# Attention and two mixers on one core: an instruction order planned in six passes from latest starts, and the first operands loaded in three parts

## The chip, the cores and the metric

The kernel runs on one core of one Trainium2 chip. The metric is the device time of one execution in microseconds (us); less is better. The engines are named as the profile names them: PE is TensorE, DVE is VectorE, ACT is ScalarE, POOL is GpSimd, SP is the queue that issues DMA transfers.

## The reference

Three stages follow each other, all in float32, for 4 batches of 448 positions. Causal attention with 12 heads of 64 (24 pairs of heads in all) gives x of 4 x 448 x 768. A mixer follows: a product over positions (token mixing) and one over channels. Then a gated one, with a normalisation and a product over positions in between.

```python
scores = scale * q @ k^T, causal mask, softmax          # 4 x 12 heads, 448 x 448
x = attn @ v                                            # 4 x 448 x 768
u = x + (relu(x^T @ w_tok1) @ w_tok2)^T                 # 448 -> 256 -> 448
x = u + relu(u @ w_ch1) @ w_ch2                         # 768 -> 1536 -> 768
h = relu(x @ w_in); u, v = halves of h                  # 768 -> 2 x 512
v_n = (v - mean(v)) / sqrt(var(v) + 1e-6)
out = (u * (w_spatial @ v_n + b_spatial)) @ w_out       # 448 x 448, 512 -> 768
```

## The kernel before

The kernel function emits no instruction directly. It first describes all work as *jobs* of a class `Plan` (a job is one or a few instructions on one engine), with what each reads and writes, an estimated duration, a priority number and, for PSUM tiles, the banks it may use. `Plan.order()` then simulates the five queues with these estimates and gives one order of all jobs, in which they are emitted; every engine executes its own share in that order.

The simulation is one pass of list scheduling. For each engine it looks for the jobs that could start first, takes of those that could start within 0.03 us the one with the smallest priority, and does the one that starts earliest over all engines, or the one of smaller priority where starts lie within 0.1 us. A job on another engine becomes ready 0.1 us after its producer (0.25 after PE, more before PE); a transfer ends after its size over 340 GB/s and a `LANDING` of 2.8 us. A PSUM tile takes a bank when its first job starts. Some jobs have a second engine, and go where they can start better: the copies of transposed probabilities and of attention outputs are for ACT, or else for DVE. Two kinds of work are marked as sharing a port between DVE and POOL and never overlap in the plan; the small reductions' statistics (L464) are not marked.

The priorities are numbers set by hand: a pair of heads has its number n (for later pairs 1e5 and a slope), token mixing 3g + 4.5, relu and residual work of the channel part -1 (always first), weight conversions and splits offsets such as `LOW + i`, `AHEAD_OF_USE`, `WEIGHT_PRIO`.

The work in order of time, with the lines that the later steps touch:

- Attention (`scores`, `transposed`, `weighted`): for a pair, PE multiplies the four causal chunks of queries (L427, tile pss); DVE masks and takes row maxima (L436, into P and stats); ACT takes exponentials (L453); DVE adds and inverts the sums (L464, L465); POOL scales (L474); PE transposes P (L511, pst), ACT or DVE copies it (L515, L514, PT); PE multiplies by v (L613, L618, pso), and ACT (L622) or DVE (L621) copies the result to U. The operands of a pair come by one transfer into one of two stage buffers (L348): 128 partitions, 448 query columns then 448 key columns.
- The token weights come in three transfers (L318) and are unpacked on DVE (L288, L290, L292: tile psw and way) and split into a high and a low part (L329 on ACT, `lo_part`, L264, on POOL or DVE). Token mixing follows (psm).
- The channel part does batches 0 and 1 with three products of split operands (L273 to L275; uhl, hid, whl) and batches 2 and 3 by a scheme of seven products (psf), whose combined operands are built by `factors`, `weight_factors` and `gather` (raw, ts, hs; L837, L881, L931) and split in two by ACT (L868, L832) and DVE or POOL (L264; fa for weights, fb for data). L1010 adds products to U.
- The gated part: values psv, hidden pairs psf, normalisation (L1122 to L1136), the product over positions (psp, L1285), bias and gate on DVE (L1292, L1293), the last products with w_out.

PE begins with two dummy matmuls on a zeroed tile (L1351) which run while the first transfer is under way. `_layout` on the host arranges the inputs.

Of the kernel before, what the change touches and what calls it, by code (L numbers as in the profile page):

```python
# [59 lines left out]
MOVE = 0  # L60
WEIGHT_PRIO = -0.7

AHEAD_OF_USE = 9.0
LEAD, SLOPE = 14.0, 2.0

LANDING = 2.8

TOK_PRIO = 1.0

# [25 lines left out]
class Plan:  # L95
# [33 lines left out]
        return j  # L129

    def order(self):
        inf = float("inf")
# [5 lines left out]
        for j in self.jobs:  # L138
            j.left = len(j.before)
            j.ready = j.at  # L140
            for p in j.before:
                p.after.append(j)
            for b in j.bufs:
                b.left = len(b.jobs)
        engines = ("PE", "ACT", "DVE", "POOL", "SP")
        free = dict.fromkeys(engines, 0.0)
        bank_free = [0.0] * 8
# [18 lines left out]
        while done < len(self.jobs):  # L166
            best = None
            for e in engines:
                if not avail[e]:
                    continue  # L170
                starts = [(start(j, e), j) for j in avail[e]]
                first = min(s for s, _ in starts)
                if first == inf:
                    continue
                s, j = min(((s, j) for s, j in starts if s <= first + 0.03), key=lambda x: (x[1].prio, x[1].index))
                if best is None or (s, j.prio) < (best[0] - 0.1, best[1].prio) or s < best[0] + 0.1 and j.prio < best[1].prio:
                    best = (s, j, e)
            s, j, e = best
            avail[j.eng].remove(j)
            if j.other:  # L180
# [21 lines left out]
            for a in j.after:  # L202
# [6 lines left out]
                a.left -= 1  # L209
                if a.left == 0:  # L210
                    add(a)
        return sorted(self.jobs, key=lambda j: (j.start, j.index))


@with_exitstack
def mixer_kernel(ctx: ExitStack, tc: tile.TileContext, qkv, wtok, wch, wgv, wsp, bsp, out):
# [126 lines left out]
    def load(n):  # L343
        st = stage[n % 2]
        operands[n] = {"st": st}
        p = n - 2.0
        src = qkv[n // NP, n % NP]
        job("SP", 0.4, lambda: nc.sync.dma_start(st.t, src[:, : 2 * S]), w=[(st, 0)], prio=p, size=458752)  # L348
        v = buf(f"v{n % 2}", [8, D], F32, "v")
        operands[n]["v"] = v  # L350
        job("SP", 0.4, lambda: nc.sync.dma_start(v.t, src[:, 2 * S :].rearrange("p (c d) -> p c d", d=D)), w=[(v, 0)], prio=p + (0.1 if n else 1.1), size=262144)
# [5 lines left out]
    def nominal(n):  # L357
        return 0.0 if n < EAGER else START + (n - EAGER) * STEP
# [13 lines left out]
    def scores(n):  # L372
# [46 lines left out]
        def mms(some):  # L419
            for i in some:  # L420
                q0, q1 = CHUNKS[i]
                W = q1
                ks = [slice(2 * S - W, 2 * S) if n < BLOCKS else slice(S, S + W), slice(S, S + W)]
                for k, (a, c) in enumerate(terms):
                    for j in range(2):
                        r = slice(64 * j, 64 * j + 64)
                        nc.tensor.matmul(ps(i, j), a.t[r, q0:q1], c.t[r, ks[j]], start=(k == 0), stop=(k == last))  # L427
# [939 lines left out]
def _layout(inputs):  # L1367
# [66 lines left out]
```

## Time and profile before

| | us |
|---|---|
| median of 3 runs | 770.83 |
| lowest and highest | 768.9 and 773.86 |
| the profiled execution | 769.79 |
| its span from first to last instruction | 768.0 |
| busy: PE, PE's weight loads | 750.4, 642.0 |
| busy: DVE, ACT, POOL | 640.4, 427.5, 299.4 |

The mean clock granted to PE was 0.995 of its full 2.4 GHz. A timeline row gives the start, the duration, the engine, the line of the kernel, the operation, the tiles written and read, shapes, and in brackets the idle time before it with what ended it. The durations of matmuls overlap: a row of 0.37 us can be followed by the next 0.21 us later.

### The profile page before, as it was taken

The numbers are of one execution on the slowest core, as the hardware profiler recorded it, in microseconds if no ns is written. First come the engines' busy times: TensorE is split into PE (matmuls) and PEld (weight loads), VectorE is DVE, ScalarE is ACT, GpSimd is POOL, SyncE is SP. The second block draws the span as 40 slices with busy tenths as digits, with TensorE's granted clock in tenths as the row PEclk, the third lists the DMA queues.
The fourth block names the chain that finished last, engine by engine and source line by source line (L and its number), as shares of the span: only waits on it lengthen the run. The fifth ranks groups of instructions, "written<-read, shape, count | busy, mean of one in ns | idle before, by whom it ended". The sixth has DMA issues, their size and how long they took to land. (4 is left out here: it accounts for less than half of the span.)

```text
span 768.0 us, 12460 instructions
## 1 busy us (share of the span) xinstructions
PE 750.4 (98%) x4216; PEld 642.0 (84%) x4216; DVE 640.4 (83%) x1517; ACT 427.5 (56%) x1035; POOL 299.4 (39%) x354
## 2 busy tenths in 40 slices
PE   8998999999999999999999999999999999999998
PEld 4576778888887888888889899998988898888997
DVE  6989899898878978787469977999999998599482
ACT  6997676743358465452337667544564675545241
POOL 4788756466647565542310000000411050653210
PEclk9999999999999999999999999999999999999999
DMA  7683676889955896998722122421401100400113
GB/s 268 199 285 115 225 260 237 305 282 344 350 182 179 255 321 207 286 254 262 219 83 113 42 83 83 149 78 42 124 14 42 42 0 1 131 1 37 73 49 131
DMA packets 48320, 122.02 MB, mean 159 GB/s; under 512 B 4864, under 2 KB 19840, under 8 KB 47744
## 3 DMA queue, kind: packets, MB, share of 16 engines
q1 hardware_dynamic: 48256, 121.23, 47.7%
q8 instruction: 33, 0.54, 0.3%
q14 instruction: 31, 0.25, 0.1%
HBM read 91.46 MB, written 29.75 MB: 158 GB/s over the span
## 5 line engine op out<-in xcount | busy, mean ns | idle before, releaser
L275 PE MATMUL psf<-fb,fa 128*128 128x448 f32 x420 | 154.6, 368 | 2.4 <-DVE fa L264 2.3
L273 PE MATMUL psf<-fb,fa 128*128 128x448 f32 x420 | 154.6, 368 | 1.7 <-DVE U L1010 1.7
L274 PE MATMUL psf<-fb,fa 128*128 128x448 f32 x420 | 154.3, 367 | 0.0
L264 POOL TENSOR_TENSOR whl<-whl 128x768 fp32r<-128x768 f32 x45 | 82.8, 1847 | 77.8 <-ACT whl L749 70.5
L453 ACT ACTIVATE P<-P,stats 128x448 f32<-128x448 f32 (+3 forms) x192 | 95.6, 503 | 25.0 <-DVE stats L436 22.6
L474 POOL TENSOR_SCALAR P<-P,stats 128x448 f32<-128x448 f32 (+2 forms) x192 | 88.0, 477 | 36.3 <-DVE stats L465 26.0
L275 PEld LDWEIGHTS psf<-fb,fa 128*128 128x128 f32 x420 | 79.3, 189 | 10.1 <-DVE fa L264 3.5
L273 PEld LDWEIGHTS psf<-fb,fa 128*128 128x128 f32 x420 | 79.3, 189 | 9.6 <-issue 2.0
L274 PEld LDWEIGHTS psf<-fb,fa 128*128 128x128 f32 x420 | 79.3, 189 | 6.8
L868 ACT CAST fa<-raw 128x384 fp32r<-128x384 f32 (+1 forms) x112 | 56.2, 531 | 46.0 <-PE psf L275 24.9
L436 DVE CUSTOM_DVE_ANT_0 P<-pss,mask 128x448 f32<-128x448 f32 (+3 forms) x192 | 70.1, 413 | 8.8 <-PE pss L427 7.4
L264 POOL TENSOR_TENSOR wv<-wf,wv 128x512 fp32r<-128x512 f32 x6 | 8.8, 1486 | 159.6 <-DVE fb L264 152.1
L264 DVE TENSOR_TENSOR fa<-raw,fa 128x384 fp32r<-128x384 f32 (+1 forms) x109 | 62.7, 600 | 6.7 <-ACT fa L868 6.7
L273 PE MATMUL ps<-hid,whl 128*128 128x448 f32 x144 | 54.7, 380 | 1.2 <-DVE hid L267 1.1
L273 PE MATMUL ps<-uhl,whl 128*128 128x448 f32 x144 | 55.3, 384 | 0.0
L275 PE MATMUL ps<-hid,whl 128*128 128x448 f32 x144 | 52.7, 366 | 0.0
L274 PE MATMUL ps<-hid,whl 128*128 128x448 f32 x144 | 52.7, 366 | 0.0
L275 PE MATMUL ps<-uhl,whl 128*128 128x448 f32 x144 | 52.7, 366 | 0.0
L274 PE MATMUL ps<-uhl,whl 128*128 128x448 f32 x144 | 52.6, 365 | 0.0
L749 ACT CAST whl<-whl 128x768 fp32r<-128x768 f32 x45 | 37.4, 834 | 24.6 <-DMA whl<-plain 24.4
L264 POOL TENSOR_TENSOR ql<-stage,qh 128x896 fp32r<-128x896 f32 x18 | 38.1, 2118 | 24.5 <-issue 12.9
L789 DVE TENSOR_TENSOR U<-ps,U 128x448 f32<-128x448 f32 x48 | 29.8, 620 | 20.6 <-PE ps L275 19.9
(174 smaller groups left out, 1813.7 us busy)
## 6 DMA issues: line engine op xcount, KB each, us to landing
way<-in_wch SPq DMA_DIRECT2D x24, 768.0 KB, 5.5
whl<-plain SPq DMA_DIRECT2D x45, 384.0 KB, 4.5
stage<-in_qkv SPq DMA_DIRECT2D x24, 448.0 KB, 3.9
plain<-way SPq DMA_DIRECT2D x24, 384.0 KB, 3.1
raw<-plain SPq DMA_DIRECT2D x24, 384.0 KB, 3.6
round<-PB SPq DMA_DIRECT2D x7, 1024.0 KB, 6.5
PT<-round SPq DMA_DIRECT2D x28, 256.0 KB, 6.3
v<-in_qkv SPq DMA_DIRECT2D x24, 256.0 KB, 3.8
```

The costliest lines, as they stand in the source:

```text
L264: e.tensor_tensor(lo, x, hi.bitcast(F32), op=ALU.subtract)
L273: nc.tensor.matmul(ps, ah, bh, start=(first and i == 0), stop=False, **kw)
L274: nc.tensor.matmul(ps, ah, bl, start=False, stop=False, **kw)
L275: nc.tensor.matmul(ps, al, bh, start=False, stop=(last and i == n - 1), **kw)
L436: nc.vector.tensor_tensor_reduce(out=P(i)[:M, j, :], in0=ps(i, j), in1=mask[:M, S - 128 : S - 128 + W] if j == 0 and n < BLOCKS or M == 64 ...
L453: nc.scalar.activation(P(i)[:M, j, :], P(i)[:M, j, :], AF.Exp, bias=s.t[:M, 0, c : c + 1], scale=-1.0, accum_out=s.t[:M, 1, c : c + 1])
L474: nc.gpsimd.tensor_scalar(P(i)[:M, j, :], P(i)[:M, j, :], s.t[:M, 2, c : c + 1], 1.0, op0=ALU.mult, op1=ALU.mult)
L749: job("ACT", act(DM, False), lambda: nc.scalar.copy(w.t[:, 0, :], w.t[:, 1, :].bitcast(F32)), r=ks, w=ks, prio=p)
L789: job("DVE", dve(S), lambda d=d, ps=ps: nc.vector.tensor_tensor(u.t[:, d, :], ps.t[:, :S], u.t[:, d, :], op=ALU.add), r=[(ps, 0), *u_keys( ...
L868: job("ACT", act(n, False), lambda: nc.scalar.copy(part(o, 0), at(d)), r=[key(d)], w=[wk], prio=p + 0.1 * o)
```

## The change

`order()` now does six passes. Each runs the same list scheduling (now `run()`); after each, `due()` walks the finished plan backwards and gives every job the latest time at which it could start without moving the plan's end: before all that depend on it (with the latencies, and for transfers size and `LANDING`), before the next owner of its PSUM bank, and for PE before the next PE job. That time replaces the priority by hand for all five engines in the next pass (jobs marked 1e8 and above keep theirs). The first pass uses the hand-set priorities; of the six plans the one with the earliest modelled end is kept. `LANDING` goes from 2.8 to 2.3.

The operands of pair 0 come in three transfers, of 384, 256 and 256 of the 896 columns. The host puts the columns that chunks 0 and 1 use side by side into the first; `scores(0)` reads them at their new places, and only chunks 3 and 2 wait for all three.

```diff
+PASSES = 6
+DUE = "ACT", "DVE", "POOL", "SP", "PE"
-LANDING = 2.8
+LANDING = 2.3
...
+        own = {j: (j.eng, j.us, j.emit, j.prio) for j in self.jobs}
+        best = None
+        for k in range(PASSES):
+            for j in self.jobs:
+                j.eng, j.us, j.emit, _ = own[j]
+            if not self.run():
+                break
+            end = max(j.start + j.us for j in self.jobs)
+            if best is None or end < best[0]:
+                best = end, [(j.start, j.eng, j.us, j.emit) for j in self.jobs], {b: b.tag for j in self.jobs for b in j.bufs if b.banks}
+            self.due(end, own, k)
...
+    def due(self, end, own, k):
...
+        late, pe = {}, end
+        for j in reversed(jobs):
+            t = pe if j.eng == "PE" else end
+            for a in j.after:
+                lat = 0.0
+                if a.eng != j.eng or j.eng == "SP":
+                    lat = 0.25 if j.eng == "PE" else 0.1
+                    if a.eng == "PE":
+                        lat += 0.3 if j.start < START else 0.8
+                if j.eng == "SP":
+                    lat += j.size / 340e3 + LANDING
+                t = min(t, late.get(a, end) - lat)
+            for b in j.bufs:
+                if j in b.jobs:
+                    for a in later.get(b, ()):
+                        t = min(t, late.get(a, end) - 0.3)
+            late[j] = t - j.us
+            if j.eng == "PE":
+                pe = late[j]
+        for j in self.jobs:
+            if own[j][0] in DUE and own[j][3] < 1e8:
+                j.prio = late[j]
...
-        job("SP", 0.4, lambda: nc.sync.dma_start(st.t, src[:, : 2 * S]), w=[(st, 0)], prio=p, size=458752)
+        for x, (c0, c1) in enumerate(((0, 2 * S),) if n else ((256, 640), (0, 256), (640, 896))):
+            job("SP", 0.4, lambda c0=c0, c1=c1: nc.sync.dma_start(st.t[:, c0:c1], src[:, c0:c1]), w=[(st, x)], prio=p, size=512 * (c1 - c0))
...
+                qs = [slice(q0, q1)] * 2
+                if n == 0:
+                    ks[0] = slice(S - W, S)
+                    q = q0 + 256 if i < 2 else q0 - 192
+                    qs = [slice(S + q0, S + q1), slice(q, q + q1 - q0)]
...
-            job("PE", us, lambda some=some: mms(some), r=split_keys, w=[*pkeys, ("scored", n, some[0])], touch=holds, prio=n, at=nominal(n))
+            job("PE", us, lambda some=some: mms(some), r=split_keys if n or some[0] == 0 else [(st, 0), (st, 1), (st, 2)], w=[*pkeys, ("scored", n, some[0])], touch=holds, prio=n, at=nominal(n))
...
+    x, a, b = pairs[0], slice(0, 64), slice(64, 128)
+    x[a, : 2 * S] = np.concatenate([x[a, S : 2 * S], x[a, :S]], axis=1)
+    x[b, :S] = np.concatenate([x[b, 192:S], x[b, :192]], axis=1)
```

The changed file has 74 more lines, so a line of before stands at a higher number after: 427 at 497, 436 at 506, 264 at 327, 288 at 351, 464 at 534, 515 at 585, 621 and 622 at 691 and 692, 837 at 907, 881 at 951, 931 at 1001, 1010 at 1080, 1292 at 1362.

PE and POOL have as many instructions as before. ACT has five more and DVE five fewer: seven copies of pso to U go from DVE to ACT, two copies of PT go the other way in the net. SP has two more. The order changes nearly everywhere. Three places on DVE follow.

First place, the second pair of heads, some 10 us after the start. Before, DVE's queue reads (pss is the scores' PSUM tile, psw and way belong to the token weights):

```order
L465 RECIPROCAL stats0_65<-stats0_65 128x4
L290 SCALAR_TENSOR_TENSOR psw_206<-way1_152,psw_206 128x384
L292 SCALAR_TENSOR_TENSOR way1_152<-way1_152,psw_206 128x384
L436 ISA P32_220,stats1_66<-pss_186,mask_64 128x448
L436 ISA stats1_66 128x1
L288 TENSOR_SCALAR psw_225<-way1_152 128x384
L290 SCALAR_TENSOR_TENSOR psw_225<-way1_152,psw_225 128x384
L292 SCALAR_TENSOR_TENSOR way1_152<-way1_152,psw_225 128x384
L436 ISA P32_220,stats1_66<-pss_188,mask_64 128x448
```

After (the 14 rows ahead of this piece hold the other six reductions of that pair):

```order
L506 ISA P101_70,stats1_66<-pss_200,mask_64 128x192
L506 ISA stats1_66 128x1
L506 ISA P101_70,stats1_66<-pss_202,mask_64 128x192
L506 ISA stats1_66 128x1
L351 TENSOR_SCALAR psw_238<-way1_154 128x384
L353 SCALAR_TENSOR_TENSOR psw_238<-way1_154,psw_238 128x384
L355 SCALAR_TENSOR_TENSOR way1_154<-way1_154,psw_238 128x384
L584 COPY PT_240<-pst_249 128x512
```

All eight reductions of the pair come ahead of the first conversion of token weights; before, the second of the eight stood behind two such conversions.

Second place, in the seven products of batches 2 and 3, at 420 us in the trace of before. Before (raw_4823 and raw_4896 belong to the weights of the next set, the last fa to those that PE takes next):

```order
L931 TENSOR_TENSOR hs_4761<-psf_4806,hs_4761 128x448
L881 TENSOR_TENSOR raw_4823<-raw_4823 128x384 x2
L881 TENSOR_TENSOR raw_4896<-raw_4823 128x384
L931 TENSOR_TENSOR hs_4842<-psf_4735,hs_4842 128x448
L264 TENSOR_TENSOR fa_4898<-raw_4823,fa_4898 128x384
L837 TENSOR_TENSOR hs_4761<-hs_4761 128x448
L837 TENSOR_TENSOR hs_4761<-hs_4842,hs_4761 128x448
L837 TENSOR_TENSOR ts_4859<-U2_2678,ts_4731 128x448
L264 TENSOR_TENSOR fa_4717<-raw_4594,fa_4717 128x384
```

After, the same split reads fa_4719<-raw_4596:

```order
L327 TENSOR_TENSOR fb_4840<-ts_4824,fb_4840 128x448
L327 TENSOR_TENSOR fb_4845<-ts_4824,fb_4845 128x448
L327 TENSOR_TENSOR fa_4719<-raw_4596,fa_4719 128x384
L327 TENSOR_TENSOR fa_4777<-raw_4708,fa_4777 128x384
L327 TENSOR_TENSOR fa_4860<-raw_4820,fa_4860 128x384
L951 TENSOR_TENSOR raw_4596<-raw_4596,raw_4708 128x384
```

The split that PE takes next stands ahead of the combinations of the next weights and of the gathers of hs, where it stood behind them.

Third place, the product over positions of the gated part (at 685 us). Before (psp is its PSUM tile, the fa of 128x768 are splits of w_out):

```order
L1292 TENSOR_TENSOR psp_7272<-psp_7272,bias_4062 128x448
L1293 TENSOR_TENSOR gate0_6369<-psp_7272,gate0_6369 128x448
L264 TENSOR_TENSOR fa_7222<-raw_7052,fa_7222 128x768
L264 TENSOR_TENSOR fa_7224<-raw_7092,fa_7224 128x768
L1292 TENSOR_TENSOR psp_7290<-psp_7290,bias_4062 128x448
L1293 TENSOR_TENSOR gate1_6409<-psp_7290,gate1_6409 128x448
```

After:

```order
L327 TENSOR_TENSOR fa_7228<-raw_7094,fa_7228 128x768
L1362 TENSOR_TENSOR psp_7272<-psp_7272,bias_4122 128x448
L1363 TENSOR_TENSOR gate0_6378<-psp_7272,gate0_6378 128x448
L1201 RECIPROCAL bias_4122<-bias_4122 128x1
L1203 TENSOR_SCALAR bias_4122<-bias_4122 128x1
L1204 TENSOR_SCALAR bias_4122<-bias_4122 128x1
L1205 TENSOR_SCALAR bias_4122<-bias_4122 128x1
L1206 TENSOR_SCALAR vn_7163<-v_7215,bias_4122 128x512
L1362 TENSOR_TENSOR psp_7289<-psp_7289,bias_4122 128x448
L1363 TENSOR_TENSOR gate1_6411<-psp_7289,gate1_6411 128x448
```

The splits, two of which stood side by side ahead of the second gate, now stand one at a time between gates (two of the four further ahead than this piece); a chain of the normalisation (bias, then vn) has come in ahead of the last gate.

## Rows read from the trace of the kernel before

**Rows 1.** Page, part 1: busy us, share of the span, instructions.

```profile
PE 750.4 (98%) x4216; PEld 642.0 (84%) x4216; DVE 640.4 (83%) x1517; ACT 427.5 (56%) x1035; POOL 299.4 (39%) x354
```

**Rows 2.** Stretches: us; PE, PEld, DVE, ACT, POOL busy; clock, DMA, GB/s.

```profile
4.15:20.00 15.85, 14.22 (x85) 8.09 (x84) 13.42 (x57) 12.39 (x42) 6.39 (x11) 1.00 0.79 289
20.00:64.00 44.00, 41.85 (x302) 28.95 (x304) 40.99 (x136) 38.03 (x119) 35.48 (x57) 1.00 0.70 234
64.00:74.00 10.00, 8.07 (x63) 6.24 (x61) 9.44 (x39) 8.57 (x28) 8.39 (x14) 0.83 0.15 36
180.00:260.00 80.00, 78.49 (x479) 67.65 (x478) 68.27 (x160) 41.13 (x97) 54.39 (x54) 1.00 0.74 254
421.00:431.00 10.00, 8.18 (x33) 7.12 (x32) 9.18 (x18) 5.04 (x10) 0.00 (x0) 0.83 0.18 62
500.00:600.00 100.00, 97.78 (x464) 86.38 (x463) 96.40 (x191) 53.90 (x120) 14.10 (x18) 1.00 0.17 55
600.00:700.00 100.00, 98.61 (x465) 86.70 (x464) 84.49 (x183) 55.09 (x119) 40.60 (x32) 1.00 0.11 34
```

**Rows 3.** What PE waited for: line, releaser, us, times, longest.

```profile
PE pss L427 <- DVE stats L436: 2.8, 4, 1.4
PE psf L275 <- DVE fa L264: 2.3, 2, 1.8
PE psf L273 <- DVE U L1010: 1.7, 1, 1.7
PE pst L511 <- ACT U L622: 0.7, 2, 0.4
```

**Rows 4.** Timeline, the start: start us, duration us, engine, line, operation.

```profile
0.73 0.86 SPq L348 DMA_DIRECT2D stage<-in_qkv  x2
3.53 0.63 PE L1351 MATMUL zeros<-P 128*128 128x256 f32 x1
4.15 2.97 PE L427 MATMUL pss<-stage 64*64 64x64 f32 x16
```

**Rows 5.** Timeline, 18 to 21 us, DVE, ACT, PE; brackets: wait before.

```profile
18.88 0.62 DVE L621 COPY U<-pso 128x448 f32<-128x448 f32 x1
19.45 0.66 ACT L453 ACTIVATE P<-P,stats 128x448 f32<-128x448 f32 x1
20.10 1.72 PE L427 MATMUL pss<-stage 64*128 64x448 f32 x8 [1.01 <-DVE stats L436]
```

**Rows 6.** L464 by tile (ns min/median/max), then timeline around 60 us.

```profile
L464 DVE TENSOR_SCALAR stats<-stats x25: 152/170/2926, 8.5 to 334.5; 128x8 f32<-128x8 f32 x23, 128x4 f32<-128x4 f32 x2
60.08 2.93 DVE L464 TENSOR_SCALAR stats<-stats 128x8 f32<-128x8 f32 x1
60.87 1.00 POOL L264 TENSOR_TENSOR whl<-way,whl 128x384 fp32r<-128x384 f32 x1
66.12 0.61 PE L427 MATMUL pss<-qh 64*128 64x448 f32 x2 [1.38 <-DVE stats L436]
```

**Rows 7.** Timeline, 420 to 426 us, DVE and PE.

```profile
420.26 1.60 DVE L881 TENSOR_TENSOR raw<-raw 128x384 f32<-128x384 f32 x3
422.79 1.35 DVE L837 TENSOR_TENSOR hs<-hs 128x448 f32<-128x448 f32 x2
425.19 0.47 PE L275 MATMUL psf<-fb,fa 128*128 128x448 f32 x1 [1.82 <-DVE fa L264]
```

**Rows 8.** Timeline, 521 to 523 us, DVE.

```profile
521.34 1.15 DVE L837 TENSOR_TENSOR hs<-hs 128x448 f32<-128x448 f32 x2
522.41 0.61 DVE L1010 TENSOR_TENSOR U<-psf,U 128x448 f32<-128x448 f32 x1
```

**Rows 9.** Timeline, 684 to 691 us, DVE and PE.

```profile
684.26 0.95 DVE L264 TENSOR_TENSOR fa<-raw,fa 128x768 fp32r<-128x768 f32 x1
686.32 2.78 DVE L264 TENSOR_TENSOR fa<-raw,fa 128x768 fp32r<-128x768 f32 x2
690.35 0.47 PE L1285 MATMUL psp<-wsp,nhl 128*128 128x448 f32 x1 [1.04 <-DVE gate L1293]
```

More of the change, by code (lines that the diff above doesn't have):

```diff
@@ L131, in order @@
     def order(self):
-        inf = float("inf")
         for j in self.jobs:
@@ L138, in order @@
         for j in self.jobs:
+            for p in j.before:
+                p.after.append(j)
+        own = {j: (j.eng, j.us, j.emit, j.prio) for j in self.jobs}
[9 more added lines that the diff above has]
+            self.due(end, own, k)
@@ new lines, in order @@
+        for j, x in zip(self.jobs, best[1]):
+            j.start, j.eng, j.us, j.emit = x
+        for b, tag in best[2].items():
+            b.tag = tag
+        return sorted(self.jobs, key=lambda j: (j.start, j.index))
+    def due(self, end, own, k):
+        jobs = sorted(self.jobs, key=lambda j: (j.start, j.index))
+        owners = {}
+        for j in jobs:
+            for b in j.bufs:
+                if b.banks and b not in owners.setdefault(b.tag, []):
+                    owners[b.tag].append(b)
+        later = {}
+        for l in owners.values():
+            for b, c in zip(l, l[1:]):
+                later[b] = [j for j in c.jobs if not j.before.intersection(c.jobs)]
+        late, pe = {}, end
[10 more added lines that the diff above has]
+                t = min(t, late.get(a, end) - lat)
+            for b in j.bufs:
+                if j in b.jobs:
[7 more added lines that the diff above has]
+                j.prio = late[j]
@@ L139, in order, with run @@
+    def run(self):
+        inf = float("inf")
+        for j in self.jobs:
             j.left = len(j.before)
             j.ready = j.at
-            for p in j.before:
-                p.after.append(j)
             for b in j.bufs:
                 b.left = len(b.jobs)
+                if b.banks:
+                    b.tag = None
         engines = ("PE", "ACT", "DVE", "POOL", "SP")
@@ L177, in order @@
                     best = (s, j, e)
+            if best is None:
+                return False
             s, j, e = best
@@ L211, in order @@
                     add(a)
-        return sorted(self.jobs, key=lambda j: (j.start, j.index))
+        return True
 @with_exitstack
@@ L426, in mms @@
                         r = slice(64 * j, 64 * j + 64)
-                        nc.tensor.matmul(ps(i, j), a.t[r, q0:q1], c.t[r, ks[j]], start=(k == 0), stop=(k == last))
+                        nc.tensor.matmul(ps(i, j), a.t[r, qs[j]], c.t[r, ks[j]], start=(k == 0), stop=(k == last))
         for some, us in (((3, 0), 1.3 if whole else 1.05), ((2, 1), 1.2 if whole else 0.9)) if n else (((0, 1), 0.9), ((3,), 1.0), ((2,), 0.7)):
             pkeys = {(banks[j][PLACE[i][0]], 0) for i in some for j in range(2)}
-            job("PE", us, lambda some=some: mms(some), r=split_keys, w=[*pkeys, ("scored", n, some[0])], touch=holds, prio=n, at=nominal(n))
+            job("PE", us, lambda some=some: mms(some), r=split_keys if n or some[0] == 0 else [(st, 0), (st, 1), (st, 2)], w=[*pkeys, ("scored", n, some[0])], touch=holds, prio=n, at=nominal(n))
         for i in chunks:
```

## The prediction, made before the changed kernel was run

> **What bounds the kernel now.** I read the page's busy times first, then the table by stretches, then the list of what TensorE waited for, then the timelines of the places where it waited. The first shows PE busy for 750.4 of 768.0 us [rows 1]: one engine carries the span, and a plan can only win what PE stands idle or runs slowly for. The stretches [rows 2] say where. Idle time is a stretch's length less its PE busy time: 1.6 us from the first score matmul at 4.15 to 20; 2.15 in 20 to 64; 1.9 in 64 to 74; 1.5 in 180 to 260; 1.8 in 421 to 431; 2.2 in 500 to 600; 1.4 in 600 to 700. In two of them the granted clock was 0.83: 10 us at 0.83 is 3.4 us at the half level (1.2 GHz), which loses 1.7 us of work each time. The rest of PE's idle time lies before 4.15 and behind its last matmul, where the plan has nothing to move. What can be won is 12.6 us of idle time and 3.4 us of slow clock, 16.0 in all.
>
> Nearly all these waits end with a VectorE instruction [rows 3]: the row maximum of the scores (L436), the split of an operand (L264), the update of U (L1010), the gate (L1293). Yet DVE is busy 83% [rows 1], so it is seldom short of time over a long stretch; something less urgent stands ahead of what PE wants. That is what an order can mend, and the argument of my forecast.
>
> **The change part by part.** The kernel does the same arithmetic on PE and POOL with the same counts. Five more copies stand on ACT and five fewer on DVE, among them seven of U that DVE made before; what counts is the order. I sum against the profiled execution, 769.8 us (span 768.0 and 1.8 around it).
>
> *Three transfers for the first pair.* PE's last warm-up matmul ends at 3.53 + 0.63 = 4.16, and the first score matmul starts at 4.15 [rows 4]. An earlier landing finds PE still warming up: 0. The bounds: -0.6, if that warm-up's end, which is modelled, really came its whole 0.63 earlier and PE stood waiting for the load; and +0.9, because two further issues (two take 0.86 [rows 4]) push the second pair's load and the transfers of values and token weights back by 0.86 on SP's queue. I take 0, since the second pair is wanted only after the first one's matmuls, at 4.15 + 2.97 = 7.1, and the first load, issued at 0.73, was there by 4.15: some 3.4 us, which from an issue at 2.0 ends at 5.4.
>
> *Up to 64 us (1.6 + 2.15 = 3.8 us idle).* The largest wait is the 1.01 at 20.10: PE waits for a reduction of DVE, which until 19.5 was busy with a copy of U (0.62) [rows 5]. The order of before mixes token-weight conversions and such copies among pair 1's reductions; after, all of that pair's reductions come first (first place of the section on the change). But in 20 to 64 ACT is busy 38.0 of 44 us and DVE 41.0 [rows 2], so a wait removed on one can come back on the other: I take 60%, -2.3, between 0 and -3.8.
>
> *64 to 74 (1.9 idle, 1.7 of clock).* The wait of 1.38 before 66.12 followed a 2.93 us standstill of a tiny DVE instruction, L464 on 128x8, while POOL ran its two-input L264 (60.87) [rows 6]; the median of L464 is 170 ns. The planner doesn't know this stall. Only a larger lead of the reductions would hide it. The new order, which puts the reductions of a pair ahead of conversions (first place), gives such a lead, but nothing in it keeps POOL's instruction away from DVE's. I take 60%: -2.2, between 0 and -3.6.
>
> *180 to 260 (1.5).* Short waits for DVE in the channel units, none of which I looked into alone; the same 60%: -0.9, between 0 and -1.5.
>
> *421 to 431 (1.8 and 1.7 of clock).* PE waits 1.82 for one split (L264). Ahead of it DVE did three combinations of the *next* weights (1.60) and two gathers of hidden parts (1.35) [rows 7]. In the new order the awaited split stands ahead of both (second place). Moving 2.95 us behind it covers the 1.82, and without the wait the half level would not appear, which in the two stretches at 0.83 stood behind these two waits, 1.38 and 1.82 (the 1.7 in 500 to 600 brought none; the clock there reads 1.00 [rows 2]). I take all of it: -3.5. The other end is 0, if what now stands ahead becomes late itself.
>
> *500 to 600 (2.2).* The update of U at 522.41, for which PE waited 1.7 [rows 3], came behind gathers worth 1.15 [rows 8]: the same pattern, 70%: -1.5, between 0 and -2.2.
>
> *600 to 700 (1.4).* The gate that PE waited 1.04 for stands behind two 768-wide splits, 2.78 together [rows 9]. In the new order two of the four splits are already done and the others come one at a time (third place); but a normalisation chain has moved in between, and the last gate of that piece stands behind it. 65%: -0.9, between 0 and -1.4.
>
> *What is added.* Copies on ACT, later drains, stalls at other places: nothing in the trace prices these, so from 0 to 6 us; nearest to one further wait like the 1.38, I take +1.5.
>
> Sum: 0 - 2.3 - 2.2 - 0.9 - 3.5 - 1.5 - 0.9 + 1.5 = -9.8, or 760.0 us for an execution like the profiled one. The median of the runs shown, 770.83, lies 1.0 above it: 761.0.
>
> A rule speaks against the third and the seventh term. The rows: L464, 170 ns at the median, took 2.93 us beside POOL's work [rows 6]; a 768-wide split took 0.95 alone and 1.39 on average for two beside POOL [rows 9]. The Trainium skill, Advanced Engine Details and Errata, VectorE Performance Modes, Mode Summary, says that VectorE's second port to SBUF is shared with GpSimd, so that two-port Vector instructions and GpSimd ones hold each other up. By that rule the trace agrees, the standstill stays wherever the two meet, and those two terms would be 0: the sum would be -6.7.
>
> **The rivals.**
> 1. *The waits only change their names.* The first 74 us and the spatial stage are short of DVE and ACT time, and there nothing is won; 421 to 431 and 500 to 600 give 3.5 + 1.5, less a new wait of 1.5: -5.0, 765.8. For it: DVE 41.0 and ACT 38.0 of 44 us [rows 2]. Against it: the waits are few and each has a plainly postponable instruction ahead.
> 2. *Slower: U's copies queue on ACT.* ACT executes in order; seven copies that DVE made now stand behind exponentials, and a transpose waits for such a copy, as PE did twice for L622 (0.7 in sum) [rows 3]. A copy took 0.62 on DVE and an exponential of 448 columns takes 0.66 [rows 5]; behind two of these a copy ends 1.94 later. Seven such delays are 13.6, two falls of the clock 3.4; only the late gains of 5.0 remain: +12.0, 782.8. It decides from (5.0 - 3.4) / 7 = 0.23 us per copy for slower at all, and from 1.3 us for over 1%. Against it: of the 13 copies that ACT makes in the kernel before only two made PE wait, 0.4 at the longest [rows 3].
> 3. *DVE's stalls beside POOL stay, or recur.* If they stay, the two terms that hang on them are lost: 761.0 + 2.2 + 0.9 = 764.1. Each further one that lands on the path costs 1.38 and 1.7 of clock, 3.1; two more give 770.3. For it: the 2.93 above, which no plan foresaw. Against it: one such stall in the whole span of before brought the clock down.
> 4. *More than the idle time.* All 16.0 us go (754.8), and PE's busy time itself shrinks where the matmuls stand apart. For it: weight loading is busy 66% in 20 to 64 (28.9 of 44) against 87% in 600 to 700 [rows 2]; at 87% the same loads would take 44 x 0.21 = 9 us less, of which I count 2: 752.8. The Trainium skill, Perfetto Trace Analysis, Identifying the Most-Contended Engine, calls matmul busy time a poor measure and weight-load time a better one; by it the early stage has room that the idle sum doesn't show. Against it: the matmuls there have other shapes (64 rows in [rows 4, 5], 128 later).
>
> That the change does not do what it says is a case for the split load alone, at 0 above; the new order is there in the built program.
>
> **How the numbers follow.** Forecast 0.46 (its own range 757 to 765), rival 1 0.26, rival 2 0.10, rival 3 0.08, rival 4 0.10. Low end 753.5: all 16.0 gone gives 754.8, and half of rival 4 lies below. High end 770.5: holds rivals 1 and 3, leaves out rival 2. About 1%, 7.7 us, is what a measurement of this kernel tells from no change: faster means under 763.1, slower over 778.5. Faster: 0.42 of the forecast's 0.46 and rival 4's 0.10, 0.52. Slower: 0.08 of rival 2's 0.10. Within 1%: the rest, 0.40.
>
> **What would show it.** Right: no granted clock of 0.83 in any stretch from 421 to 431 and 64 to 74; the 1.8 for L264's split and the 1.7 for U gone from PE's waits; PE idle sum near 8 us instead of 17.6; first score matmul still at 4.15. Wrong: PE waiting over 3 us in sum for ACT's U copies (rival 2); new waits of over 1 us for output drains after 600; L464 again near 3 us just before a PE wait (rival 3); a PE busy time that differs from 750 by more than the 3.4 of clock, which no term explains.

## The result and the profile after

| | before | after |
|---|---|---|
| median, us | 769.87 (4 runs) | 761.50 (4 runs) |
| lowest and highest | 768.44, 773.86 | 758.74, 766.71 |
| profiled execution, its span | 769.79, 768.0 | 762.46, 760.7 |
| idle time of PE in the span | 17.6 | 13.5 |

The ratio is 0.989, with a 95% interval of 0.9857 to 0.9923: 8.4 us, or 1.1%, faster. In the runs of the experiments below the kernel before had medians of 770.4 to 771.6. Of the four executions after, two ran at a mean granted clock of 1.000 (758.74 and 760.54 us), the profiled one at 0.997 and the slowest at 0.995.

The busy times on the page of after, to be held against [rows 1]:

```profile
PE 747.2 (98%) x4216; PEld 640.3 (84%) x4216; DVE 622.3 (82%) x1512; ACT 427.4 (56%) x1040; POOL 298.2 (39%) x354
```

The span is 7.3 us shorter: PE is idle 4.1 us less (768.0 - 750.4 = 17.6 before, 760.7 - 747.2 = 13.5 after) and busy 3.2 us less. DVE is busy 18 us less with five instructions fewer; the group of L464, 12.7 us before with its standstills, takes 7.4 for the same 23 instructions.

The table by stretches of after, with the columns of [rows 2] (length; PE, PEld, DVE, ACT, POOL busy; clock; DMA; GB/s), and two stretches that were free of idle time before:

```profile
4.15:20.00 15.85, 14.92 (x93) 8.59 (x92) 13.47 (x58) 12.30 (x45) 7.89 (x16) 1.00 0.66 250
20.00:64.00 44.00, 42.33 (x320) 30.03 (x316) 41.08 (x147) 42.21 (x130) 37.72 (x61) 1.00 0.74 243
64.00:74.00 10.00, 10.00 (x89) 7.46 (x88) 9.77 (x35) 8.62 (x26) 8.67 (x12) 1.00 0.81 251
74.00:180.00 106.00, 105.72 (x696) 87.59 (x693) 92.04 (x245) 65.04 (x171) 61.23 (x75) 1.00 0.73 246
180.00:260.00 80.00, 76.74 (x457) 65.19 (x456) 64.42 (x160) 44.30 (x107) 51.95 (x50) 0.98 0.83 274
421.00:431.00 10.00, 10.00 (x50) 8.98 (x49) 9.52 (x21) 7.54 (x17) 0.00 (x0) 1.00 0.01 3
431.00:500.00 69.00, 68.37 (x337) 62.97 (x337) 59.91 (x117) 42.39 (x90) 0.00 (x0) 1.00 0.27 98
500.00:600.00 100.00, 99.43 (x471) 88.02 (x471) 97.93 (x207) 53.24 (x120) 14.04 (x18) 1.00 0.16 50
600.00:700.00 100.00, 99.10 (x470) 87.67 (x470) 83.31 (x168) 56.38 (x120) 40.87 (x33) 1.00 0.12 38
```

Read against [rows 2], as length less PE busy time: 4.15 to 20, 1.6 to 0.9; 20 to 64, 2.15 to 1.7; 64 to 74, 1.9 to 0; 74 to 180, 0 to 0.3; 180 to 260, 1.5 to 3.3, and the clock there is below 1; 421 to 431, 1.8 to 0; 431 to 500, 0 to 0.6; 500 to 600, 2.2 to 0.6; 600 to 700, 1.4 to 0.9. The two stretches at a clock of 0.83 are at 1.00. So in the two profiled executions the change won where the forecast said, except in 180 to 260, where it lost 1.8; 0.9 more went in the two stretches that had been free.

What PE waited for in after, to be held against [rows 3] (a selection):

```profile
PE ps L336 <- DVE hid L330: 1.9, 1, 1.9
PE ps L336 <- DVE U L859: 1.2, 2, 1.1
PE psp L1355 <- DVE gate L1363: 0.9, 2, 0.7
PE psf L336 <- DVE U L1080: 0.6, 1, 0.6
PE pss L497 <- DMA stage<-in_qkv: 0.5, 1, 0.5
PE pst L581 <- ACT U L692: 0.3, 1, 0.3
```

The 1.8 for the split of weights and the four waits for reductions are gone from the top. Two groups of waits for channel units (hid and U) have taken their place, 1.9 and 1.1 at the longest. ACT's copies of U, the road to the slower side, make PE wait 0.3 once.

The two new waits are the interesting ones. The timeline of after around the longer of them, DVE and then PE:

```profile
209.07 0.56 DVE L351 TENSOR_SCALAR psw<-way 128x384 uint32<-128x384 uint32 x1 [1.15 <-DMA way<-in_wch]
210.98 0.56 DVE L355 SCALAR_TENSOR_TENSOR way<-way,psw 128x384 uint32<-128x384 uint32 x1 [0.75 <-DMA plain<-way]
211.45 0.62 DVE L330 SCALAR_TENSOR_TENSOR hid<-ps,hid 128x448 fp32r<-128x448 f32 x1
...
212.13 0.47 PE L336 MATMUL ps<-hid,whl 128*128 128x448 f32 x1 [1.94 <-DVE hid L330]
214.47 0.58 PE L338 MATMUL ps<-hid,whl 128*128 128x448 f32 x1
```

DVE's rows stand in the order of its queue. At 209.07 it begins a conversion of channel weights after standing 1.15 us for the transfer that brings them; at 210.98 it stands 0.75 again, for the store of the converted half before. The relu remainder that PE needs (L330, hid) is queued behind, and PE waits 1.94. The second PE row shows what can follow such a wait: from 213 to 216 us a matmul takes 0.58 instead of 0.36, the half level of the clock. The 1.05 at 194.9 is the same picture with a wait of DVE for gated weights (0.92), without a fall of the clock.

Why were those weights late? DVE's conversions (tile psw) between 68 and 101 us, before and then after:

```profile
68.00:101.00 33.00, 11.48 (x22) 0.96 0.53 180
```

```profile
68.00:101.00 33.00, 1.14 (x3) 1.00 0.35 103
```

22 instructions before, 3 after. In the plan of after, PE's first channel unit starts as filler at 69.5 us, and its PSUM tile takes bank 7, which it holds until the unit is complete near 100 us. Bank 7 is the only one that the conversions 0 to 7 may use. In the plan of before the unit starts at 93 us and its tile takes bank 6. So for 33 us hardly a weight is converted, and the lead that the kernel before had is missing 100 us later. Experiment 5 tests this; experiment 12, which has the same gap, shows that its price is not fixed.

### The profile page after: what moved, and what is told of

Read it like the earlier page. It is cut to its first block, busy times and chain, and to the rows that moved or that the text cites. A ratio compares the mean times of both kernels' runs of the same rounds, so it can differ in the third digit from the quotient of the medians.

```text
span 760.7 us, 12440 instructions
## 1 busy us (share of the span) xinstructions
PE 747.2 (98%) x4216; PEld 640.3 (84%) x4216; DVE 622.3 (82%) x1512; ACT 427.4 (56%) x1040; POOL 298.2 (39%) x354
## 5 line engine op out<-in xcount | busy, mean ns | idle before, releaser
L544 POOL TENSOR_SCALAR P<-P,stats 128x448 f32<-128x448 f32 (+3 forms) x192 | 88.3, 483 | 38.1 <-DVE stats L535 30.8
L327 DVE TENSOR_TENSOR fa<-raw,fa 128x384 fp32r<-128x384 f32 (+1 forms) x109 | 61.0, 585 | 7.1 <-ACT fa L938 7.1
L336 PE MATMUL ps<-hid,whl 128*128 128x448 f32 x144 | 55.2, 383 | 3.1 <-DVE hid L330 1.9
L338 PE MATMUL ps<-hid,whl 128*128 128x448 f32 x144 | 53.3, 370 | 0.0
L337 PE MATMUL ps<-hid,whl 128*128 128x448 f32 x144 | 53.3, 370 | 0.0
L327 POOL TENSOR_TENSOR ql<-stage,qh 128x896 fp32r<-128x896 f32 x18 | 38.1, 2116 | 14.9 <-issue 11.7
## 6 DMA issues: line engine op xcount, KB each, us to landing
way<-in_wch SPq DMA_DIRECT2D x24, 768.0 KB, 5.7
```

The lines of the kernel that those rows point to most:

```text
L327: e.tensor_tensor(lo, x, hi.bitcast(F32), op=ALU.subtract)
L336: nc.tensor.matmul(ps, ah, bh, start=(first and i == 0), stop=False, **kw)
L337: nc.tensor.matmul(ps, ah, bl, start=False, stop=False, **kw)
L338: nc.tensor.matmul(ps, al, bh, start=False, stop=(last and i == n - 1), **kw)
L544: nc.gpsimd.tensor_scalar(P(i)[:M, j, :], P(i)[:M, j, :], s.t[:M, 2, c : c + 1], 1.0, op0=ALU.mult, op1=ALU.mult)
```

## The experiments

All ran with five rounds beside the kernel before. Its median moved between 769.9 and 771.6 from one set of runs to the next, so a difference of 1 or 2 us between the medians of two experiments says nothing.

**1. The three transfers alone.** The kernel before with the lines of the change that split the first load (and the host's columns), nothing else:

```diff
-        job("SP", 0.4, lambda: nc.sync.dma_start(st.t, src[:, : 2 * S]), w=[(st, 0)], prio=p, size=458752)
+        for x, (c0, c1) in enumerate(((0, 2 * S),) if n else ((256, 640), (0, 256), (640, 896))):
...
```

> The kernel before with nothing but the first pair's three transfers. My theory (the early landing is hidden behind PE's warm-up, as the first term of the sum has it): within 1 us of before, first score matmul within 0.1 us of 4.15. Rival (the start is worth something): 1 to 2 us faster and PE's idle time up to 20 us smaller by as much. A third possibility: since the plan is made anew, other waits move; then the difference lies behind 20 us and comes with other names in PE's waits.

Measured: 798.17 us, ratio 1.0349 (1.0327 to 1.0371). The first two expectations failed. The third, other waits behind 20 us, is what came, at a size that nobody had named: 27 us slower. PE's waits, the stretch where most of them lie, and DVE's conversions (tile psw) from 72 to 109 us:

```profile
PE ps L273 <- DVE U L795: 10.2, 6, 2.7
PE ps L273 <- DVE hid L267: 5.2, 2, 2.8
PE ps L273 <- DVE way L292: 4.1, 1, 4.1
```

```profile
180.00:260.00 80.00, 60.74 (x271) 51.94 (x269) 64.14 (x122) 23.22 (x42) 37.95 (x29) 0.89 0.83 291
```

```profile
72.00:109.00 37.00, 1.24 (x4) 0.97 0.31 93
```

19 of 80 us idle, against 1.5 before [rows 2]. Two more transfers on SP shift the plan's first steps by under a microsecond; in the plan that comes out PE's first channel unit takes bank 7 (by the plan from 76 to 104 us), four instructions of conversions fall in 37 us, and the weights come too late for PE. The hand-set priorities did not keep the bank free, and the latest starts of the changed kernel didn't either.

**2. LANDING alone.**

```diff
-LANDING = 2.8
+LANDING = 2.3
```

> The kernel before with LANDING 2.3 for 2.8 and nothing else, one pass with the priorities by hand. My theory (the gain comes from the latest starts): within 4 us of before, the two places with the clock at 0.83 or others like them still there. Rival (any new number shuffles the plan and 8 us are within what a shuffle does): 5 to 10 us off in either direction.

Measured: 768.15, ratio 0.9967 (0.9951 to 0.9984). Within the 4 us of my theory; the clock fell near 66 and 425 us as before. Though small, 2.9 us is clear of the noise.

**3. One pass.**

```diff
-PASSES = 6
+PASSES = 1
```

> The changed kernel with PASSES 1: three transfers and LANDING 2.3, but the order by the priorities set by hand. My theory: 768 to 773 us, all of the gain gone, idle time of PE near 17 us. Rival (transfers and LANDING made the gain): 760 to 764.

Measured: 768.20, ratio 0.9972 (0.9953 to 0.9992), at the edge of my range: most of the gain is gone, not all. PE's idle time is 19.0 us. The six passes are worth 6.7 us (768.2 - 761.5), transfers and LANDING 2 to 3. The waits of PE behind 400 us stand in the same jobs as before:

```profile
423.41 0.47 PE L338 MATMUL psf<-fb,fa 128*128 128x448 f32 x1 [1.82 <-DVE fa L327]
541.29 0.44 PE L336 MATMUL psf<-fb,fa 128*128 128x448 f32 x1 [0.90 <-DVE U L1080]
579.69 0.47 PE L338 MATMUL psf<-fb,fa 128*128 128x448 f32 x1 [1.08 <-DVE fa L327]
686.50 0.47 PE L1355 MATMUL psp<-wsp,nhl 128*128 128x448 f32 x1 [0.98 <-DVE gate L1363]
```

Two things differ. The wait of 1.82 is back, but here no fall of the clock followed it (1.00 in 421 to 431, 0.83 before). And 64 to 74 us is free of idle time at a clock of 1.00 with one pass already, so the gain there does not need latest starts.

**4. Six passes, the first load in one piece.**

```diff
-        for x, (c0, c1) in enumerate(((0, 2 * S),) if n else ((256, 640), (0, 256), (640, 896))):
+        for x, (c0, c1) in enumerate(((0, 2 * S),)):
...
-            job("PE", ... r=split_keys if n or some[0] == 0 else [(st, 0), (st, 1), (st, 2)], ...
+            job("PE", ... r=split_keys if n or some[0] == 0 else split_keys, ...
```

> The changed kernel with the first pair's operands in one transfer as before, six passes kept (columns in the new order, all chunks wait for the one transfer). My theory: 760 to 764, as the changed kernel, with a first score matmul at 4.15. Rival (the split load counts): 764 to 768.

Measured: 766.97, ratio 0.9942 (0.9925 to 0.9959). The number fits the rival, its reason doesn't: the start is no worse (first score matmul at 4.09, as in the changed kernel), and most of PE's idle time lies between 20 and 400 us, among others in waits for copies of PT and for xs that the changed kernel's plan doesn't have. Compare the stretches to 400 and behind it:

```profile
4.15:400.00 395.85, 385.05 (x2482) 313.11 (x2482) 317.67 (x900) 233.32 (x627) 232.79 (x282) 1.00 0.78 246
400.00:755.00 355.00, 353.93 (x1697) 317.66 (x1696) 305.37 (x609) 192.25 (x409) 62.47 (x57) 1.00 0.18 63
```

Before 400 us it is idle 10.8 us, after 1.1. It is another plan, not another start.

**5. A second bank for the conversions.** The changed kernel with

```diff
-        convert(... (7,) if i < 8 else (3,), keep=i)
+        convert(... (7,) if i < 5 else (7, 3) if i < 8 else (3,), keep=i)
```

> The changed kernel, with the channel weights' conversions 5 to 7 allowed bank 3 beside bank 7. My theory: in the changed kernel PE's first channel unit, begun as filler at 69.5 us, takes bank 7 until 97.5 and so keeps DVE from converting weights from 68 to 101 us; 100 us later DVE stands waiting for weight transfers and PE waits 1.05 at 194.9 and 1.94 at 212.1 with a fall of the clock (1.7). With the second bank the conversions go on from 68 to 101, these two waits go, and the time falls by 3 to 5 us, to 756 to 759. Rival (transfers are late because they are ordered by latest start and land later than planned): the waits near 195 to 215 stay, 760 to 763.

Measured: 761.20, ratio 0.9869 (0.9846 to 0.9892). The mechanism held: DVE converts through the 33 us (24 instructions instead of 3), the waits near 195 and 212 are gone, and 180 to 260 is free of idle time. The gain of 3 to 5 us did not come, and the time lies in the rival's range without its reason; what was won went into 74 to 180:

```profile
74.00:180.00 106.00, 102.86 (x655) 85.07 (x652) 89.13 (x233) 61.98 (x162) 54.27 (x62) 1.00 0.79 259
180.00:260.00 80.00, 79.99 (x518) 67.51 (x517) 66.20 (x179) 50.58 (x125) 59.52 (x63) 1.00 0.79 272
```

There PE now waits 3.1 us, the longest for POOL:

```profile
135.68 1.09 PE L581 MATMUL pst<-ident,P 128*128 128x128 f32 x8 [1.28 <-POOL P L544]
```

**6. The same bank in the first experiment.**

> The first experiment (kernel before with the three transfers, 798 us) with the same second bank for conversions 5 to 7. My theory (its 27 us are the same bank: no conversion from 72 to 109 us, then PE waiting over 17 us for weights between 184 and 243): most of the loss goes, 768 to 776, and the waits between 184 and 243 sum to under 4 us. Rival (the three transfers themselves delay everything behind them): 790 or more.

Measured: 774.41, ratio 1.0037 (1.0022 to 1.0052), 24 us less than without the second bank. The stretch of 180 to 260 is idle 1.6 instead of 19.3:

```profile
180.00:260.00 80.00, 78.44 (x524) 64.35 (x521) 66.00 (x185) 52.28 (x137) 57.60 (x63) 1.00 0.69 229
```

```profile
72.00:109.00 37.00, 17.44 (x32) 1.00 0.77 253
```

The first channel unit takes bank 7 here too, but the conversions go on in bank 3, 32 instructions instead of 4. So the bank is the cause of 24 of the 27 us. That is as far as one edit can show it, since it makes another plan as well. In the changed kernel the same gap stands ahead of 3 us of waiting and a fall of the clock.

**7. Latest starts for DVE alone.**

```diff
-DUE = "ACT", "DVE", "POOL", "SP", "PE"
+DUE = ("DVE",)
```

> The changed kernel with latest starts for VectorE's jobs alone; the other four engines keep the priorities set by hand. My theory (DVE's order is the lever): the waits behind 400 us go as in the changed kernel (for the split near 421, the update of U near 541, the split near 580), 761 to 766 us. Rival (all engines must be planned together, ACT's and PE's order too): those waits stay, 766 to 770.

Measured: 765.65, ratio 0.9931 (0.9907 to 0.9954). The waits near 421, 541 and 580 are gone; of the 6.7 us of the passes DVE's order alone gives 2.5. Behind 400 us PE is idle 2.9, against 2.1 in the changed kernel and 5.2 with one pass; what is left are waits for gates and operands behind 677 us. So most of the late gain is DVE's order. Where the rest of the time comes from is not isolated, since this is another plan before 400 us as well.

**8. LANDING 2.2 in the changed kernel.**

```diff
-LANDING = 2.3
+LANDING = 2.2
```

> The changed kernel with LANDING 2.2 for 2.3, a number without meaning of its own at this size. If the gain is a property of the method (latest starts in six passes), 759 to 764. My theory, after the shuffles seen so far, is that about half of it belongs to this one plan: 764 to 770, with the waits behind 400 us still gone (they go by latest starts) and other waits in the first 260 us.

Measured: 773.24, ratio 1.0042 (1.0018 to 1.0066): slower than the kernel before, and worse than both expectations. A shift of a tenth of a microsecond in an estimate takes away more than the whole gain. Its stretches:

```profile
4.15:400.00 395.85, 386.24 (x2475) 313.60 (x2475) 313.17 (x894) 234.30 (x628) 232.55 (x282) 1.00 0.77 247
400.00:755.00 355.00, 352.70 (x1687) 315.53 (x1687) 307.61 (x613) 191.03 (x406) 55.12 (x57) 1.00 0.18 62
```

Behind 400 us PE is idle 2.3 us, as in the changed kernel (2.1). Before 400 it is idle 9.6 (6.4 in the changed kernel), with 1.6 and 1.8 near 204 and 210; the 10.7 us that L351 stood for weights compare with 4.2 in the changed kernel. The larger part of the difference is PE's busy time, 752.5 us, 5.3 more than in the changed kernel at nearly the same clock. Its matmuls are no longer (the largest group takes 368 ns, 367 in the changed kernel), so they start further apart; what holds them I did not find. The other executions ran at granted clocks down to 0.991, which is part of their spread (770.6 to 777.9).

**9. LANDING 2.2 with the second bank.** Both edits.

> The same LANDING 2.2 with the second bank for conversions 5 to 7. My theory (the second bank takes away what makes the first 260 us depend on luck): 759 to 764, within 2 us of the run with two banks and LANDING 2.3 (761.2). Rival (plans scatter with or without it): 5 us or more away from 761.

Measured: 768.47, ratio 0.9962 (0.9940 to 0.9985); 7 us above 761.2, so the rival holds. It is 4.8 less than with one bank. The bank is one source of the scatter, not the only one.

**10. Two banks for conversions 6 and 7, twelve passes.**

```diff
-PASSES = 6
+PASSES = 12
...
-        convert(... (7,) if i < 8 else (3,), keep=i)
+        convert(... (7,) if i < 6 else (7, 3) if i < 8 else (3,), keep=i)
```

> The changed kernel with the second bank for conversions 6 and 7 alone and twelve passes instead of six, the version meant to beat it. My theory: 756 to 760, no wait over 1 us of PE from 180 to 260 and no clock below full there. Rival (what is won in one place is lost in another, as with the second bank and six passes): 760 to 763.

Measured: 761.55, ratio 0.9876 (0.9854 to 0.9899): level with the changed kernel, the rival's range. In 180 to 260 the longest wait is 0.63 and the clock full, as my theory had it; 74 to 180 is idle 2.5 us instead of 0.3. No version tried beats the changed kernel by more than the noise. Two of DVE's waits for weights are worth a look, with what came behind the second (DVE, then PE):

```profile
94.89 0.56 DVE L351 TENSOR_SCALAR psw<-way 128x384 uint32<-128x384 uint32 x1 [2.83 <-DMA way<-in_wch]
142.91 0.56 DVE L351 TENSOR_SCALAR psw<-way 128x384 uint32<-128x384 uint32 x1 [1.56 <-DMA way<-in_wch]
144.58 1.01 DVE L327 TENSOR_TENSOR xs<-psm,xs 128x384 fp32r<-128x384 f32 x2
145.65 0.44 PE L767 MATMUL psm<-xs,wt 128*128 128x384 f32 x1 [1.54 <-DVE xs L327]
```

DVE stood 8.4 us for channel weights in all, from 84 to 162 us. The longest stand, 2.83, made no wait of PE. The one of 1.56 did: the split of xs that PE wants is queued behind that conversion, and PE waits 1.54. A stand costs where something that PE wants soon is queued behind it.

**11 and 12. Latest starts behind 395 us alone, and before it alone.** Jobs are told apart by their start in the first pass:

```diff
+SPLIT = 395.0
...
+            if k == 0:
+                self.first = {j: j.start for j in self.jobs}
...
-            if own[j][0] in DUE and own[j][3] < 1e8:
-                j.prio = late[j]
+            if own[j][3] < 1e8 and self.first[j] >= SPLIT:
+                j.prio = 1e6 + late[j]
```

That is experiment 11, late only. Experiment 12, early only, has in place of the last two lines:

```diff
+            if own[j][3] < 1e8:
+                j.prio = late[j] if self.first[j] < SPLIT else 1e6 + own[j][3]
```

> The run with one pass (768.2 us) plus latest starts for those jobs alone that it places at 395 us or later (six passes as in the changed kernel); up to there DVE's and PE's orders are the same as with one pass. My theory (the late gain is the part that belongs to the method): the waits near 423, 541, 580 and 687 sum to 5.2 us with one pass and go down to about 1.5; 763 to 765.5. Rival (the gain lies in the attention and channel part): 767 or more.

> The counterpart: latest starts for the jobs placed before 395 us, priorities by hand behind it. Up to there the orders are those of the changed kernel. My theory: its early part as the changed kernel's, the four late waits back (about 5 us, and a fall of the clock where the one of 1.8 returns), 765 to 768. Rival (the early part holds the whole gain): 760 to 763.

Measured: late only 764.53, ratio 0.9899 (0.9873 to 0.9925); early only 764.93, ratio 0.9902 (0.9872 to 0.9931). By the medians each gives about half of what six passes give over one (768.2): 3.7 and 3.3 of 6.7 us. By the ratios to the kernel before, which ran beside each of them, it is more, 5.6 and 5.4 of 6.3. So each part counts for itself; that the two add up to the whole is not shown. The stretches to 400 us and behind it, one pass, late only, early only:

```profile
4.15:400.00 395.85, 387.02 (x2505) 318.49 (x2505) 322.46 (x903) 236.72 (x636) 232.81 (x282) 1.00 0.77 247
400.00:755.00 355.00, 349.81 (x1683) 314.83 (x1682) 305.98 (x600) 192.57 (x407) 63.72 (x57) 1.00 0.18 63
...
4.15:400.00 395.85, 386.25 (x2499) 317.44 (x2499) 320.62 (x900) 236.65 (x636) 232.76 (x282) 1.00 0.77 247
400.00:755.00 355.00, 352.97 (x1697) 317.50 (x1696) 304.07 (x605) 190.50 (x406) 62.73 (x57) 1.00 0.18 63
...
4.15:400.00 395.85, 390.47 (x2519) 320.78 (x2519) 321.18 (x912) 235.72 (x633) 233.25 (x282) 1.00 0.77 248
400.00:755.00 355.00, 349.76 (x1675) 314.82 (x1675) 304.70 (x597) 191.71 (x405) 63.64 (x57) 1.00 0.18 62
```

Behind 400 us PE is idle 5.2 us with one pass, 2.0 with latest starts there and 5.2 again without. Before 400 us it is 8.8 with one pass, 9.6 late only, 5.4 early only. The rival of each run falls; early only lies a hair below my own range.

Experiment 12 shows one thing more. Up to 391 us every engine's order in it is that of the changed kernel, with the same 3 instructions of conversions from 68 to 101 us, and yet in 180 to 260 PE is idle 1.6 us at a clock of 1.00, where the changed kernel lost 3.3 and had a fall. The wait of 1.05 is missing, and of the 1.94 this is left:

```profile
211.78 0.47 PE L339 MATMUL ps<-hid,whl 128*128 128x448 f32 x1 [1.18 <-DVE hid L333]
```

DVE stood 0.69 and 0.76 us ahead of it instead of 1.15 and 0.75. So one and the same order can lose 1.6 us there, or 3.3 and a fall of the clock. Over the whole stretch to 400 us the two differ by 1.0 us of idle time, and one pass and late only, which also share their orders so far, by 0.8; a smaller difference between two profiles says nothing. Behind 400 us the changed kernel and late only (2.1 and 2.0) agree, and one pass and early only (5.2 and 5.2).

**The plan's own estimate.** `order()` works out a modelled end for the plan that it keeps, without any chip. It is 758.1 us for the kernel before, 749.1 for the changed one, 783.4 for experiment 1 and 756.5 for experiment 8. Of the 27 us of experiment 1 the model so has 25, and of the 11.7 between LANDING 2.3 and 2.2 it has 7.4: the larger part of the scatter arises in the planner and not on the chip. The model does not tell all: experiments 4 and 9 are modelled within 2 us of the changed kernel (750.1 and 750.8) and measured 5.5 and 7.0 above it, and experiment 10 has the earliest end of all (746.6) and is level.

## Why the prediction was right, and where it was not

The forecast was 761.0 and the median is 761.5. That they lie so close is in part luck. The change was forecast at 9.8 us, and it is 8.4 between the medians and 7.3 between the profiled executions; the forecast then added 1.0, because the median of before known at the time, 770.83, lay above its profiled execution, and one run more brought it down to 769.87. Step by step, in profiled times (769.8 to 762.5; the profiled execution of after lies 1.0 above its median):

- *Three transfers, 0.* Right as to the landing: the first score matmul stands at 4.09 instead of 4.15, and at 4.09 with the load in one piece too (experiment 4). The other side of the edit shows as well:

```profile
4.09 1.18 PE L497 MATMUL pss<-stage 64*64 64x64 f32 x8
5.77 1.56 PE L497 MATMUL pss<-stage 64*128 64x448 f32 x8 [0.50 <-DMA stage<-in_qkv]
```

  PE then waits 0.50 for the other parts and reaches the second pair at 7.48 instead of 7.31 (7.18 in experiment 4), within the bounds. What the term left out is that the edit moves the plan: 5.5 us between experiment 4 and the changed kernel, 27 in experiment 1.
- *Up to 64 us, -2.3.* Measured -1.2 of idle time (3.8 to 2.6): half. PE's waits for DVE there went from 1.4 us to 0.2, and 0.5 for the first pair's loads came new. Its waits for ACT and POOL, 1.1 each before, are 1.1 and 0.7: they did not grow, though ACT is busy 42.2 of 44 us now, 38.0 before [rows 2]. The term took 60% of all idle time there, and only 1.4 of the 3.8 us was for DVE.
- *64 to 74, -2.2.* Measured -3.6, the whole wait and its clock. The reason is not shown to be mine: experiment 3 has the stretch free as well, with one pass and the priorities by hand.
- *180 to 260, -0.9.* The waits that were there are gone, all 1.5 of them; the 3.3 that stand there now are new and belong to the term of what is added.
- *421 to 431, -3.5.* Right for the two profiled executions: 1.8 and the clock's 1.7. Experiment 3 has the wait back, experiment 11 is free of it. The clock's part is less sure than its term: the same wait was followed by a fall in experiment 12 (1.83, clock 0.83) and by none in experiment 3. And a fall costs less than the 1.7 that I took. Of the 74 executions of the kernel before that ran beside the experiments, 17 had a mean granted clock of 0.999 or more and a median of 769.7 us, 32 had 0.995 or 0.996, as the profiled one with its two falls, and a median of 771.5: 1.8 us for two falls, not 3.4. What makes up for the rest is not shown.
- *500 to 600, -1.5; 600 to 700, -0.9.* Measured -1.65 and -0.5. The second was cut by the chain that I had named, and its rows are these, DVE, PE, and what POOL did beside:

```profile
675.68 1.26 DVE L1206 TENSOR_SCALAR vn<-v,bias 128x512 f32<-128x512 f32 x1
...
677.51 0.62 DVE L1363 TENSOR_TENSOR gate<-psp,gate 128x448 f32<-128x448 f32 x1
...
678.19 0.47 PE L1355 MATMUL psp<-wsp,nhl 128*128 128x448 f32 x1 [0.66 <-DVE gate L1363]
...
675.51 1.15 POOL L327 TENSOR_TENSOR fb<-gate,fb 128x448 fp32r<-128x448 f32 x1 [0.87 <-ACT fb L902]
```

  The last step of the normalisation (vn) stands ahead of the gate's two instructions, and PE waits 0.66. Vn took 1.26 us beside POOL's split, where its median over 14 is 0.55. The 0.71 more would cover the whole 0.66. It looks like a stall of DVE beside POOL, as rival 3 had them, but no run separates it: at 681.06, with POOL at work as well, vn took 0.55.
- *Added, +1.5.* This is the term that was mis-sized most: 3.3 in 180 to 260, the half clock behind it (213 to 216, about 1.7 as at the two places before), 0.6 at 452 and 0.3 at 87 make 5.9, near the upper end of 6 that I had kept for the range. "One further wait like the 1.38" was the wrong neighbour. I had looked at what DVE does ahead of PE's work, and not at which transfer DVE itself would stand for once its conversions were put off. Against these 4.4 beyond the term, and 1.5 missing up to 64 and in 600 to 700, 64 to 74 gave 1.4 more than its term, 180 to 260 gave 0.6 more, and PE's busy time fell by 1.5 beyond what the clock explains, for which I have no cause. That leaves the sum about 2.5 short: -7.3 for -9.8. With other landings the term is smaller (1.6 in 180 to 260 and no fall in experiment 12). The sign I had named, idle time near 8 us, did not come: it is 13.5.

Rival 1 (the waits only change their names) was wrong for the first 74 us, which gave 4.8 us, and right in that new waits came, larger ones than the 1.5 that it had. Rival 2 (ACT's copies) is out: 20 copies, PE waited for one, 0.3. Rival 3 (DVE's stalls beside POOL) may hold for one place, the 0.66 at 678.19. L464 still stands, 7.4 us in its group and 1.70 at the longest, but none of its standstills came ahead of a wait of PE. Rival 4 (more than the idle time) did not come, 13.5 us of idle time are left; the 1.5 us less of busy time point its way.

By the rule that I weighed against two terms (the Trainium skill, Advanced Engine Details and Errata, VectorE Performance Modes, Mode Summary: two-port Vector instructions and GpSimd ones hold each other up) both should have been 0. The trace agrees that such stalls go on, and one of them may decide in 600 to 700; it disagrees in 64 to 74, where the whole wait went.

What the prediction got right for a reason is the late half. Every plan with latest starts behind 400 us left PE 0.8 to 2.9 us idle from 400 to 755 (experiments 4, 5, 7 to 11, the changed kernel), every plan without them 5.2 or more (before, experiments 1 to 3, 6 and 12). The early half is the property of one plan: PE's idle time to 400 us is 6.4 with LANDING 2.3 and 9.6 with 2.2, and the times are 761.5 and 773.2. I gave 0.08 to slower, and that was fair only because the built order was there to be read; of the six plans with latest starts on all engines throughout, one, experiment 8, came out slower than the kernel before.

## What to carry to other kernels

Priorities by latest start put first what the bounding engine waits for. Behind 400 us, where the work is much the same from unit to unit, that gain stayed under every constant tried here (LANDING, passes, banks); that the sameness is the reason was not tested. Where a planner is greedy, any small edit can make another plan: judge an edit together with two or three neighbours of its constants before crediting it, compare the plans' own modelled ends first, which cost no run, and read the built order. A scarce buffer (here one PSUM bank) that filler work can take is a hidden dependence of everything else that must pass through it; look for a stretch where a whole kind of instruction is missing.

## What was not expected of the hardware

A wait of DVE for a transfer has no price of its own: in experiment 10 one of 2.83 us made no wait of PE and one of 1.56 made a wait of 1.54; in the changed kernel 1.15 and 0.75 together made one of 1.94. And the same stores of 384 KB from SBUF (plain<-way, 24 of them) landed after 3.1 us at the median before and after 6.7 in the changed kernel. This goes with the plan of the early transfers: 6.0 to 7.0 in the seven kernels in which they go by latest starts, 2.9 to 3.8 in the seven in which they don't. What holds them is not shown; the plan's single figure for a landing can't hold for both.
